# Contracting the last 64 channels over 128 rows in a split-precision MLP and DFT chain

## The chip, the cores and the metric

The kernel runs on one NeuronCore of a Trainium2 chip. The metric is the device time of one execution in microseconds. Engines are named as in the profile: PE is the matmul engine (PEld its weight loads), DVE, ACT and POOL are the vector, scalar and GpSimd engines, SP issues most of the DMAs.

## The reference

The program is a chain of three blocks over 2 batches, 768 tokens and 320 channels (8 heads of 40).

```
attention:  gated linear recurrence over 768 steps, 8 heads x 40   -> x [2, 768, 320]
block 1:    h = relu(x^T w_tok1) w_tok2 ;  u = x + h^T
            out1 = u + relu(u w_ch1) w_ch2          w_ch1 [320, 1536], w_ch2 [1536, 320]
block 2:    u = x + real(fft(fft(x, tokens), channels))
            un = layernorm(u) ;  out = u + relu(un w_ch1) w_ch2     w_ch1 [320, 1280]
```

Weights are handed over as float64 bits.

## The kernel before, in words

**Number format.** Every product that matters is done with each operand split in two: a high part rounded to 12 bits and a low part, the rest. A product is then three matmuls, high by high, high by low and low by high; low by low is left out. The weight words are decoded and split on the chip: `decode` (lines 73 to 87) is one ACT and three DVE instructions on a piece, `split` (94 to 99) adds one ACT copy that rounds to the high part and one POOL subtraction that gives the low part. The pool of decoded pieces has three buffers.

**The 320 channels as contraction rows.** 320 is 128 + 128 + 64. The activations of two token tiles (256 tokens) are transposed on PE and split by `transpose2` (409 to 425) into `uT`, five slots of 128 rows by 256 columns: slots 0 and 1 are the high parts of channels 0 to 255, slots 2 and 3 their low parts; slot 4 holds the high parts of channels 256 to 319 in rows 0 to 63 and their low parts in rows 64 to 127. The weight pieces of class `FF1` (110 to 136) have three row tiles; the third is rows 256 to 319 of the matrix twice, one copy above the other. So one matmul of 128 rows, high weights twice against slot 4, gives high by high and high weight by low activation together. The third term, low weight by high activation, needs 64 rows only. `split` forms the low part of that third row tile for rows 0 to 63 alone (`rows=64` from `FF1.conv`, line 126), and `mlp_hidden` (428 to 447) issues as the last of each group of eight matmuls one that contracts over 64 rows, `g(2, 1, ff, 64)` against `uT[0:64, 4, :]` (line 442).

**Loops.** Each of the two MLPs works on six sets of two token tiles, three per batch. A set is `mlp_hidden`, groups of eight matmuls of 256 columns, one group for each 128 hidden features (12 in block 1, 10 in block 2), two groups to a PSUM bank `phid`; `relu_split` (390) turns a bank into the high and low halves of `hid` with one ACT and one DVE instruction; then `mlp_out` (449) contracts `hid` with `w2` for each token tile, 36 or 30 matmuls of 320 columns into `pout`, all of 128 rows. In all there are 2 x 3 x 12 + 2 x 3 x 10 = 132 groups of eight. The DFT along the channels (`dft_stage`, 490 to 522) uses the same slots: for each of 3 tile pairs of each batch there are two groups of eight matmuls, the last of which contracts over 64 rows (line 515), 12 such groups. Its cosine and sine tables come as one constant, 128 rows high; slot 5 of it, the low parts of rows 256 to 319, fills rows 0 to 63 and is zero below (line 825).

**Order.** The generators `ch_stage`, `moe2_stage`, `dft_stage` and `attn_batch` yield estimated durations; `merge` emits a side stage under a main one (attention of batch 1 under the first MLP stage, the DFT of batch 0 under the second, that of batch 1 under the third), and a scheduler then orders each engine's instructions by its own simulated times. The order on each engine is fixed in the program: an engine waits at an instruction whose input is late, whatever stands behind it. PSUM pool `pmm` has four banks, shared by `phid`, `pout` and others. The weights of block 1 are decoded while its first set runs; those of block 2's first matrix (`v1`) under block 1's second stage, as their raw words land; those of its second matrix (`v2`) reuse the buffers of block 1's `w2` and can be loaded only as these come free.

Of the kernel before, what the change touches and what calls it, by code (L numbers as in the profile page):

```python
# [21 lines left out]
DM = H * D  # L22
# [16 lines left out]
def body(ctx, tc, io, out):  # L39
# [29 lines left out]
    def mm(o, l, r, a, z):  # L69
        nc.tensor.matmul(o, l, r, start=a, stop=z)  # L70

# [1 line left out]
    def decode(raw, n, dst=None):  # L73
        """float32 of the n float64 words in raw: the sign, the exponent less 896, 23 bits."""
        z = pz.tile([128, RAW], F32, tag="z", name="z")
        wi = raw.bitcast(I32).rearrange("p (n two) -> p n two", two=2)
        wf = raw.bitcast(F32).rearrange("p (n two) -> p n two", two=2)
        hw, lw = wi[:, :n, 1], wi[:, :n, 0]
        zi = z.bitcast(I32)[:, :n]
        nc.scalar.activation(z[:, :n], wf[:, :n, 1], AF.Copy, scale=2.0 ** -112)  # L80
        nc.vector.tensor_scalar(hw, hw, -2147483648, None, op0=ALU.bitwise_and)  # L81
        nc.vector.scalar_tensor_tensor(  # L82
            hw, zi, 3, hw, op0=ALU.logical_shift_left, op1=ALU.bitwise_or)
        o = zi if dst is None else dst.bitcast(I32)
        nc.vector.scalar_tensor_tensor(  # L85
            o, lw, 29, hw, op0=ALU.logical_shift_right, op1=ALU.bitwise_or)
        return z[:, :n]
# [3 lines left out]
        dma(raw, src)  # L91
        return raw

    def split(pool, tag, raw, n, rows=128):
        z = decode(raw, n)
        w = pool.tile([128, 2, n], F32R, tag=tag, bufs=1, name="w")
        nc.scalar.activation(w[:, 0, :], z, AF.Copy)  # L97
        nc.gpsimd.tensor_tensor(w[:rows, 1, :], z[:rows], f(w[:rows, 0, :]), op=ALU.subtract)  # L98
        return w

    def tok_load(i):
# [6 lines left out]
        decode(raw, RAW, tokw[:, i * RAW:(i + 1) * RAW])  # L108

    class FF1:  # L110
        """[DM, nf] in pieces: three row tiles (the third is rows 256.. twice) by RAW columns."""

        def __init__(self, pool, tag, src, nf):
            self.pool, self.tag, self.src = pool, tag, src
# [8 lines left out]

        def conv(self, i):
            k = self.keys[i]
            self.w[k] = split(self.pool, f"{self.tag}_{i}", self.raw.pop(k), self.n[k[0]],
                              64 if k[1] == 2 else 128)

        def ensure(self, ff):
            while len(self.w) < len(self.keys) and self.keys[len(self.w)][0] <= 128 * ff:  # L130
                self.conv(len(self.w))

        def get(self, kt, hl, ff, rows=128):
            o = 128 * ff
            s = o // RAW * RAW
            return self.w[s, kt][:rows, hl, o - s:o - s + 128]

    class FF2:
        """[nk * 128, DM] in pieces of 128 rows."""

        def __init__(self, pool, tag, src, nk):
            self.pool, self.tag, self.src, self.nk = pool, tag, src, nk
# [12 lines left out]
        def get(self, hl, k):  # L155
            return self.w[k][:, hl, :]

# [1 line left out]
    def gates(early, bcast, loadg):  # L159
        gt = ph.tile([128, 6144], F32R, tag="hid", name="gt")  # L160
        g = f(gt)
# [82 lines left out]

        return store

# [1 line left out]
    def attn_init(pa, pas):  # L248
        st = {}
        st["C"] = [pa.tile([128, 4, 2 * V41], F32, tag=f"C{i}", bufs=1, name=f"C{i}")  # L250
# [21 lines left out]
        st[b, c][2] = Dt  # L272

    def attn_chunk(pa, pas, st, b, c):
        """Yields in stages so that chunks can be pipelined."""
        kvo, kq, Dt, *pg = st[b, c]
        k3 = kvo[:, 0:DM].rearrange("p (h d) -> p h d", d=D)
        v3 = kvo[:, DM:DM + H * V41].rearrange("p (h d) -> p h d", d=V41)
# [126 lines left out]
            mm(p, tk2[:, m, 128 * t:128 * t + 128], hs[:, m, :], m == 0, m == 1)  # L405
        nc.vector.tensor_tensor(us[b][:, t, :], us[b][:, t, :], p, op=ALU.add)

# [1 line left out]
    def transpose2(ta, tb, pool=pu, tag="uT", bufs=2):  # L409
        uT = pool.tile([128, 5, 256], F32R, tag=tag, bufs=bufs, name="uT")  # L410
        pp, tg = late.get("pt", (pmm, "mm"))
# [12 lines left out]
            uT[64:128, 4, :], p2[0:64, 0:256], f(uT[0:64, 4, :]), op=ALU.subtract)  # L424
        return uT

# [1 line left out]
    def mlp_hidden(uT, wt, nff, w2=None):  # L428
        hid = ph.tile([128, 12, 2, 256], F32R, tag="hid", name="hid")
        for f2 in range(nff // 2):  # L430
            wt.ensure(2 * f2 + 4)
            if w2 is not None:
                w2.ensure(2 * (f2 - nff // 2 + 2))
            p = pmm.tile([128, 512], F32, tag="mm", name="phid").rearrange(
                "p (k n) -> p k n", k=2)
            for q in range(2):
                ff = 2 * f2 + q
                g = wt.get
                ops = [(g(0, 0, ff), uT[:, 0, :]), (g(1, 0, ff), uT[:, 1, :]),
                       (g(0, 1, ff), uT[:, 0, :]), (g(1, 1, ff), uT[:, 1, :]),  # L440
                       (g(0, 0, ff), uT[:, 2, :]), (g(1, 0, ff), uT[:, 3, :]),
                       (g(2, 0, ff), uT[:, 4, :]), (g(2, 1, ff, 64), uT[0:64, 4, :])]
                for i, (l, r) in enumerate(ops):
                    mm(p[:, q, :], l, r, i == 0, i == 7)
            relu_split(hid[:, 2 * f2:2 * f2 + 2, 0, :], hid[:, 2 * f2:2 * f2 + 2, 1, :], p)
            yield 1740
        return hid
# [38 lines left out]
            for i in range(2):  # L486
                yield from mlp_out(hid, W2, 12, us[b][:, ORDER[k][i], :], i)

# [1 line left out]
    def dft_stage(b, pf, pfs):  # L490
        cds, css, alt, odd = late["cds"], late["css"], late["alt"], late["odd"]
        n0 = NS + 2 * NJ
# [11 lines left out]
        for i in range(3):  # L504
            eT = eo(i)
            yield 700
            p = pfs.tile([128, 512], F32, tag="f", name="pf1")
            no = NS + NJ if i == 0 else NS
            for o, lsl, r0, n in ((0, 128, 0, no), (no, 0, NS, NJ)):
                ls = slice(lsl, lsl + 128)  # L510
                rs = slice(r0, r0 + n)
                ops = [(eT[:, 0, ls], cds[:, 0, rs]), (eT[:, 1, ls], cds[:, 1, rs]),
                       (eT[:, 2, ls], cds[:, 0, rs]), (eT[:, 3, ls], cds[:, 1, rs]),
                       (eT[:, 0, ls], cds[:, 2, rs]), (eT[:, 1, ls], cds[:, 3, rs]),
                       (eT[:, 4, ls], cds[:, 4, rs]), (eT[0:64, 4, ls], cds[0:64, 5, rs])]
                for q, (l, r) in enumerate(ops):
                    mm(p[:, o:o + n], l, r, q == 0, q == 7)
            nn = no + NJ
            nc.scalar.activation(AB[i][:, 0, 0:nn], p[:, 0:nn], AF.Copy)
            nc.vector.tensor_tensor(  # L520
                AB[i][:, 1, 0:nn], p[:, 0:nn], f(AB[i][:, 0, 0:nn]), op=ALU.subtract)
            yield 1800
# [15 lines left out]
        for k in range(3):  # L538
# [32 lines left out]
            nc.gpsimd.tensor_tensor(u[:, k, :], u[:, k, :], mx[:, 0:DM], op=ALU.add)  # L571
            nc.gpsimd.tensor_tensor(u[:, 3 + k, :], u[:, 3 + k, :], r2, op=ALU.add)
            yield 2100
        # layer norm statistics
        mv = pf.tile([128, 6, 2], F32, tag="mv", bufs=2, name="mv")
        for t in (0, 3, 1, 4, 2, 5):
            bs = pf.tile([128, 6], F32, tag="bs", bufs=2, name="bs")
# [45 lines left out]
            pass  # L623

    def merge(main, side, mt, sd, fns=()):
        """Emit main; spread side and the small jobs evenly beneath it."""
        tm_, ts_, nf = 0.0, 0.0, 0
        done = False
        for w in main:
            tm_ += w  # L630
            fr = tm_ / mt
            while not done and ts_ < fr * sd:
                try:
                    ts_ += next(side)
                except StopIteration:
                    done = True
            while nf < len(fns) and nf < fr * len(fns):
                fns[nf]()
                nf += 1
        if not done:  # L640
            drain(side)
        while nf < len(fns):
            fns[nf]()
            nf += 1
# [4 lines left out]
    pw = pmm.tile([128, 512], F32, tag="mm", name="pwarm")  # L649

    def warm(n):
        """Keeps the tensor engine's clock up where it would idle."""
        for _ in range(n):
            mm(pw[:, 0:256], wt[:, 0:128], wt, True, True)

    # ================= program =================
    warm(16)
    pa_cm = tc.tile_pool(name="pa", bufs=2)
    pa = pa_cm.__enter__()
# [143 lines left out]
def _constants():  # L803
    c = {}
    c["ident"] = np.eye(128, dtype=np.float32)
    sel = np.zeros((B, 4, 2, 2, B, 4), np.float32)
    for b in range(B):
        for r in range(4):
            for j in range(2):
                sel[b, r, j, j, b, r] = 1.0  # L810
    c["sel"] = sel.reshape(16, 16)
    d = np.arange(DM, dtype=np.float64)[:, None]
    cd = np.zeros((DM, NJ))
    sd = np.zeros((DM, NS))
    j = np.arange(NS + 1)
    cd[:, :NS + 1] = np.cos(2 * np.pi * ((d * j) % DM) / DM)
    j = np.arange(1, NS)
    sd[:, :NS - 1] = np.sin(2 * np.pi * ((d * j) % DM) / DM)
    hi, lo = _hl(np.concatenate([sd, cd], 1))
    n = NS + NJ  # L820
    cds = np.zeros((128, 6, n), np.float32)
    cds[:, 0], cds[:, 1] = hi[0:128], hi[128:256]
    cds[:, 2], cds[:, 3] = lo[0:128], lo[128:256]
    cds[0:64, 4], cds[64:128, 4] = hi[256:], hi[256:]
    cds[0:64, 5] = lo[256:]
    k = np.arange(384)
    a = 2 * np.pi * ((k[:, None] * k[None, :]) % S) / S
    cs, ss = np.cos(a), np.sin(a)
    cs[0, :] = (k % 2 == 0)
    ss[0, :] = 0.0  # L830
    css = np.zeros((128, 4, 3, 384), np.float32)
    for q, m in ((0, cs), (2, ss)):
        hi, lo = _hl(m)
        css[:, q] = hi.reshape(3, 128, 384).transpose(1, 0, 2)
        css[:, q + 1] = lo.reshape(3, 128, 384).transpose(1, 0, 2)
    alt = np.zeros((128, 256), np.float32)
    alt[:, 0] = 1.0 - 2.0 * (np.arange(128) % 2)
    alt[0, 128:] = np.arange(128) % 2
    c["dft"] = np.ascontiguousarray(
        np.concatenate([css.reshape(128, -1), alt, cds.reshape(128, -1)], 1))  # L840
    c["idx"] = np.ascontiguousarray((_slots()[384:] - 384).reshape(3, 128).T.astype(np.int32))
    return c
# [57 lines left out]
```

## Time and profile before

| what | us |
|---|---|
| median of 3 runs | 464.22 (463.49 to 472.81) |
| span of the profiled execution | 465.3 |
| PE busy in it | 453.8 |
| DVE busy in it | 248.1 |
| ACT busy in it | 158.1 |
| POOL busy in it | 112.0 |

The profile is one execution of the program with a record for each instruction. Of that execution the page gives the span, from the first to the last instruction, which is 1.1 us above the median time of the runs; sums are made against the span and then moved by that difference. A group of instructions stands on one line by code line, engine, operation, tiles and shape; the program's matmuls all go through one helper (line 70), so they are told apart by their tiles. Ends of matmuls are modelled, and a matmul's recorded duration overlaps its neighbour's, so how fast PE goes is read from the distance between starts. Some matmul records are missing.

### The profile page before, as it was taken

To read this page: it belongs to the slowest core of one execution; us is meant where nothing else is said; L and a number is where in the kernel's file an instruction comes from. 1 tells how busy PE (TensorE), PEld (TensorE's weight loads), DVE (VectorE), ACT (ScalarE), POOL (GpSimd) and SP (SyncE) were. 2 spreads that over 40 slices of the span, in tenths; PEclk is the share of its full clock that TensorE was granted. 3 is DMA by queue.
4 is the path that set the end of the run, shared out by engine and by line. 5 is a ranking of instruction groups with operands and counts; after the bars stand their busy time and mean duration, and the time that the engine had idled before them with its cause. 6 is when DMAs were issued, how large, how long until landed. Compare 5 with 4: busy or idle time off the path is not lost.

```text
span 465.3 us, 8110 instructions
## 1 busy us (share of the span) xinstructions
PE 453.8 (98%) x3254; PEld 391.8 (84%) x3254; DVE 248.1 (53%) x515; ACT 158.1 (34%) x382; POOL 112.0 (24%) x131
## 2 busy tenths in 40 slices
PE   9899998999999999999999999979999999999996
PEld 7789876888889889778988998968989989797986
DVE  8656779899844232165892425288534235312221
ACT  2766635596454020033462212145122021202020
POOL 5574347486511002001240210022201110000000
PEclk9965599999999999999999999989999999999999
DMA  7558659933320001059100000340000000000000
GB/s 217 188 186 278 226 186 356 334 140 117 117 89 1 14 16 43 15 189 394 57 3 0 2 1 0 96 187 1 14 15 1 30 1 28 1 28 1 30 1 28
DMA packets 15669, 42.27 MB, mean 91 GB/s; under 512 B 2080, under 2 KB 4992, under 8 KB 15504
## 3 DMA queue, kind: packets, MB, share of 16 engines
q1 hardware_dynamic: 15200, 37.30, 23.6%
q0 software_dynamic: 432, 4.46, 2.4%
q8 instruction: 25, 0.41, 0.4%
q14 instruction: 12, 0.10, 0.1%
HBM read 38.76 MB, written 3.00 MB: 90 GB/s over the span
## 4 chain that ended last, share of the span: by engine, by line
PE 91%; DMA 4%; DVE 3%; issue 1%; ACT 1%; SPq 0%; DVEq 0%; ACTq 0%
PE phid L70 38%; PE pout L70 25%; PE pf L70 6%; PE ps L70 5%; PE py L350 4%; PE py L327 3%; PE pt L70 2%; PE ptr L416 2%; PE h L70 2%; DMA kq<-in_kqT_dram 1%; DMA tkr<-in_tok_dram 1%; DMA raw<-in_v_dram 1%; PE kv L70 1%; PE pwarm L70 1%; PE ptr L419 1%
## 5 line engine op out<-in xcount | busy, mean ns | idle before, releaser
L70 PE MATMUL phid<-uT,w 128*128 128x256 f32 (+1 forms) x1056 | 182.8, 308 | 3.6 <-ACT uT L420 3.6
L70 PEld LDWEIGHTS phid<-uT,w 128*128 128x128 f32 (+1 forms) x1056 | 145.0, 190 | 36.2 <-ACT uT L420 4.3
L70 PE MATMUL pout<-w,hid 128*128 128x320 f32 x792 | 126.2, 313 | 0.0
L70 PEld LDWEIGHTS pout<-w,hid 128*128 128x128 f32 x792 | 116.5, 188 | 2.7
L392 DVE SCALAR_TENSOR_TENSOR hid<-phid,hid 128x512 fp32r<-128x512 f32 x66 | 45.5, 690 | 77.3 <-ACT hid L391 77.1
L391 ACT ACTIVATE hid<-phid 128x512 fp32r<-128x512 f32 x66 | 39.4, 598 | 133.3 <-PE phid L70 131.2
L98 POOL TENSOR_TENSOR w<-z,w 128x320 fp32r<-128x320 f32 (+4 forms) x46 | 46.3, 1016 | 89.3 <-ACT w L97 89.2
L459 DVE TENSOR_TENSOR us<-us,pout 128x320 f32<-128x320 f32 x24 | 11.6, 486 | 51.6 <-PE pout L70 51.5
L97 ACT ACTIVATE w<-z 128x320 fp32r<-128x320 f32 (+2 forms) x46 | 22.0, 481 | 22.8 <-DVE z L85 22.8
L85 DVE SCALAR_TENSOR_TENSOR z<-raw 128x320 int32<-128x320 int32 (+2 forms) x46 | 29.4, 640 | 0.7
L70 PE MATMUL ps<-kq 40*128 40x128 f32 x192 | 29.5, 340 | 0.0
L80 ACT ACTIVATE z<-raw 128x320 f32<-128x320 f32 (+2 forms) x46 | 22.9, 505 | 17.8 <-DMA raw<-in_v_dram 11.9
L82 DVE SCALAR_TENSOR_TENSOR raw<-z,raw 128x320 int32<-128x320 int32 (+2 forms) x46 | 28.3, 623 | 0.4
L70 PEld LDWEIGHTS ps<-kq 40*128 40x128 f32 x192 | 24.5, 232 | 2.8 <-issue 2.1
L302 ACT ACTIVATE Dt<-Dt,tm 128x128 f32<-128x128 f32 x80 | 25.1, 393 | 0.1
L81 DVE TENSOR_SCALAR raw<-raw 128x320 int32<-128x320 int32 (+2 forms) x46 | 21.6, 473 | 6.6 <-ACT z L80 6.5
L571 POOL TENSOR_TENSOR us<-us,mx 128x320 f32<-128x320 f32 x6 | 5.5, 921 | 73.4 <-DVE mx L559 73.4
L303 POOL TENSOR_SCALAR_AFFINE_SELECT Dt<-Dt 128x512 f32<-128x512 f32 x24 | 17.9, 752 | 11.3 <-ACT Dt L302 11.2
L319 DVE TENSOR_TENSOR Dt<-Dt,ps 128x512 f32<-128x512 f32 x24 | 16.1, 679 | 7.6 <-PE ps L70 5.6
L70 PE MATMUL pwarm<-wt 128*128 128x256 bf16 x116 | 18.5, 320 | 1.1 <-DVE wt L647 1.1
L350 PEld LDWEIGHTS py<-kvo,Dt 128*64 128x64 f32 x384 | 16.2, 166 | 3.4 <-issue 2.0
L420 ACT ACTIVATE uT<-ptr 128x512 fp32r<-128x512 f32 x18 | 10.7, 594 | 24.6 <-PE ptr L416 23.5
(120 smaller groups left out, 433.3 us busy)
## 6 DMA issues: line engine op xcount, KB each, us to landing
kvo<-in_kvo_dram SPq DMA_DIRECT2D x12, 484.0 KB
Dt<-Gd SPq DMA_DIRECT2D x10, 512.0 KB
raw<-in_w_dram SPq DMA_DIRECT2D x12, 384.0 KB
kq<-in_kqT_dram SPq DMA_DIRECT2D x24, 160.0 KB
raw<-in_w_dram SPq DMA_DIRECT2D x12, 320.0 KB
raw<-in_v_dram SPq DMA_DIRECT2D x9, 384.0 KB
dc<-in_dft_dram POOLq DMA_DIRECT2D x1, 3398.0 KB, 12.9
raw<-in_v_dram SPq DMA_DIRECT2D x10, 320.0 KB
```

The source lines that it names most:

```text
L70: nc.tensor.matmul(o, l, r, start=a, stop=z)
L80: nc.scalar.activation(z[:, :n], wf[:, :n, 1], AF.Copy, scale=2.0 ** -112)
L81: nc.vector.tensor_scalar(hw, hw, -2147483648, None, op0=ALU.bitwise_and)
L82: nc.vector.scalar_tensor_tensor(hw, zi, 3, hw, op0=ALU.logical_shift_left, op1=ALU.bitwise_or)
L85: nc.vector.scalar_tensor_tensor(o, lw, 29, hw, op0=ALU.logical_shift_right, op1=ALU.bitwise_or)
L97: nc.scalar.activation(w[:, 0, :], z, AF.Copy)
L98: nc.gpsimd.tensor_tensor(w[:rows, 1, :], z[:rows], f(w[:rows, 0, :]), op=ALU.subtract)
L302: nc.scalar.activation(Dt[:, h, :], G4[j][:, r, :], AF.Exp, bias=nu[:, h:h + 1])
L303: nc.gpsimd.affine_select(D4[:, j], D4[:, j], pattern=[[0, 4], [1, L]], compare_op=ALU.is_ge, fill=0.0, base=0, channel_multiplier=-1)
L350: nc.tensor.matmul(py[64 * q:64 * q + 64, h, :], Dt[:, h, 64 * q:64 * q + 64], v3[:, h, :], start=c == 0 and h == 0, stop=True, skip_group ...
L391: nc.scalar.activation(hi, ps, AF.Relu)
L392: nc.vector.scalar_tensor_tensor(lo, ps, 0.0, f(hi), op0=ALU.max, op1=ALU.subtract)
```

## The change

The third row tile's low part is formed for all 128 rows, so that both copies of the low weights are there, and the last matmul of each group of eight contracts over 128 rows: low weights twice against slot 4. That adds low weight by low activation for the last 64 channels. The DFT does the same; its constant gets the low table in rows 64 to 127 too. Comments and docstrings go as well; these are left out below.

```diff
-    def split(pool, tag, raw, n, rows=128):
+    def split(pool, tag, raw, n):
         z = decode(raw, n)
         w = pool.tile([128, 2, n], F32R, tag=tag, bufs=1, name="w")
         nc.scalar.activation(w[:, 0, :], z, AF.Copy)
-        nc.gpsimd.tensor_tensor(w[:rows, 1, :], z[:rows], f(w[:rows, 0, :]), op=ALU.subtract)
+        nc.gpsimd.tensor_tensor(w[:, 1, :], z, f(w[:, 0, :]), op=ALU.subtract)
...
-            self.w[k] = split(self.pool, f"{self.tag}_{i}", self.raw.pop(k), self.n[k[0]],
-                              64 if k[1] == 2 else 128)
+            self.w[k] = split(self.pool, f"{self.tag}_{i}", self.raw.pop(k), self.n[k[0]])
...
-        def get(self, kt, hl, ff, rows=128):
+        def get(self, kt, hl, ff):
             o = 128 * ff
             s = o // RAW * RAW
-            return self.w[s, kt][:rows, hl, o - s:o - s + 128]
+            return self.w[s, kt][:, hl, o - s:o - s + 128]
...
-                       (g(2, 0, ff), uT[:, 4, :]), (g(2, 1, ff, 64), uT[0:64, 4, :])]
+                       (g(2, 0, ff), uT[:, 4, :]), (g(2, 1, ff), uT[:, 4, :])]
...
-                       (eT[:, 4, ls], cds[:, 4, rs]), (eT[0:64, 4, ls], cds[0:64, 5, rs])]
+                       (eT[:, 4, ls], cds[:, 4, rs]), (eT[:, 4, ls], cds[:, 5, rs])]
...
-    cds[0:64, 5] = lo[256:]
+    cds[0:64, 5], cds[64:128, 5] = lo[256:], lo[256:]
```

## Rows read from the trace of the kernel before

**Rows 1.** Page: busy time by engine; granted PE clock in 40 slices, in tenths.
```profile
PE 453.8 (98%) x3254; PEld 391.8 (84%) x3254; DVE 248.1 (53%) x515; ACT 158.1 (34%) x382; POOL 112.0 (24%) x131
...
PEclk9965599999999999999999999989999999999999
```

**Rows 2.** Page: the chain of work that ended last, share of the span by engine.
```profile
PE 91%; DMA 4%; DVE 3%; issue 1%; ACT 1%; SPq 0%; DVEq 0%; ACTq 0%
```

**Rows 3.** Groups of PE by shape: line, operation, tiles, shapes, count | busy us, mean ns.
```profile
L70 PE MATMUL phid<-uT,w 128*128 128x256 f32 x924 | 149.2, 298 | 3.6 <-ACT uT L420 3.6
...
L70 PE MATMUL phid<-uT,w 64*128 64x256 f32 x132 | 49.9, 379 | 0.0
...
L70 PE MATMUL pf<-dc,uT 64*128 64x162 f32 x6 | 2.0, 338 | 0.0
```

**Rows 4.** Timeline of PE around one group's end: start us, us, what, how many.
```profile
440.10 0.28 PE L70 MATMUL phid<-uT,w 128*128 128x256 f32 x1
...
440.30 0.70 PE L70 MATMUL phid<-uT,w 64*128 64x256 f32 x2
...
440.62 0.51 PE L70 MATMUL phid<-uT,w 128*128 128x256 f32 x2
...
440.84 0.53 PE L70 MATMUL phid<-uT,w 128*128 128x256 f32 x3
```

**Rows 5.** Timeline of PE: one whole set of ten groups and what follows.
```profile
416.64 13.29 PE L70 MATMUL phid<-uT,w 128*128 128x256 f32 x80
429.86 0.66 PE L416 MATMUL ptr<-ident,un 128*128 128x128 f32 x4
```

**Rows 6.** Timeline of PE: a run in which all matmuls have 128 rows.
```profile
393.81 3.10 PE L70 MATMUL phid<-uT,w 128*128 128x256 f32 x24 [0.58 <-ACT uT L420]
396.75 0.60 PE L416 MATMUL ptr<-ident,un 128*128 128x128 f32 x4
```

**Rows 7.** Timeline of PE: DFT along channels (first pair), along tokens (second pair).
```profile
233.66 2.25 PE L70 MATMUL pf<-dc,uT 128*128 128x160 f32 x14
235.84 0.41 PE L70 MATMUL pout<-w,hid 128*128 128x320 f32 x1
...
251.57 2.72 PE L70 MATMUL pf<-AB,dc 128*128 128x162 f32 x20
254.12 0.32 PE L70 MATMUL phid<-uT,w 128*128 128x256 f32 x1
```

**Rows 8.** Groups of POOL by shape, the subtraction that gives the low weights.
```profile
L98 POOL TENSOR_TENSOR w<-z,w 128x384 fp32r<-128x384 f32 x14 | 15.7, 1130 | 20.4 <-ACT w L97 20.4
...
L98 POOL TENSOR_TENSOR w<-z,w 64x384 fp32r<-64x384 f32 x7 | 8.1, 1164 | 19.4 <-ACT w L97 19.4
```

**Rows 9.** Stretches: busy us of PE, PEld, DVE, ACT, POOL; PEclk, DMA share, GB/s.
```profile
76.20:123.00 46.80, 46.80 (x376) 38.84 (x374) 44.58 (x78) 32.53 (x84) 30.59 (x33) 1.00 0.61 211
221.50:245.00 23.50, 23.50 (x158) 21.31 (x157) 20.60 (x43) 12.20 (x29) 8.91 (x10) 1.00 0.06 21
304.70:329.00 24.30, 23.36 (x141) 20.48 (x142) 22.34 (x44) 12.72 (x30) 8.18 (x9) 0.93 0.14 55
```

**Rows 10.** Matmuls on `phid` in 76.2:129, 202.7:245 and 304.7:329, with their forms.
```profile
L70 PE MATMUL phid<-uT,w x129: 274/282/522, 76.2 to 128.8; 128*128 128x256 f32 x113, 64*128 64x256 f32 x16
...
L70 PE MATMUL phid<-uT,w x139: 277/282/522, 202.7 to 244.5; 128*128 128x256 f32 x122, 64*128 64x256 f32 x17
...
L70 PE MATMUL phid<-uT,w x80: 274/284/457, 305.6 to 323.9; 128*128 128x256 f32 x70, 64*128 64x256 f32 x10
```

**Rows 11.** Timeline of ACT at 220; in brackets idle before and what ended it.
```profile
220.26 0.60 ACT L391 ACTIVATE hid<-phid 128x512 fp32r<-128x512 f32 x1 [2.68 <-PE phid L70]
220.75 1.42 ACT L80 ACTIVATE z<-raw 128x384 f32<-128x384 f32 x3
```

**Rows 12.** Waits of 304.7:329 (us, times, longest); the chain after that wait.
```profile
PE phid L70 <- ACT uT L420: 3.0, 1, 3.0
...
305.64 3.66 PE phid L70 x16
```

## Prediction

> **What bounds the kernel now.** I read the page first: PE is busy for 453.8 of 465.3 us, DVE for 248.1, and the PE clock is granted in full in nearly every slice [rows 1]. A busy PE need not be a fast one, so the chain of waits comes next: 91% of the chain that ended last is PE's own work [rows 2]. The time is therefore the sum of the distances between the starts of PE's instructions, and the question is what those distances are. The groups by shape show that the 132 matmuls with 64 rows are not cheaper than their 924 neighbours with 128 rows and the same 256 columns: their mean is 379 ns against 298 [rows 3]. These durations are modelled, so I went to the timeline of single instructions. A 128-row matmul starts at 440.10, the 64-row one at 440.30, the next 128-row one at 440.62 and the one after that at 440.84, after which three share 0.53 us [rows 4]. Steps of 0.20, 0.32 and 0.22 us stand around every 64-row matmul. What a step is without one is seen in a run where the scheduler put 24 matmuls of 128 rows together: from 393.81 to the next instruction at 396.75 [rows 6], 2.94 us. That run has one slow step of the 0.22 kind, after its wait; without the 0.10 it has too much, a step is 2.84 / 24 = 0.118 us.
>
> The same rows speak on the cause. The first slow step, 0.20 us, lies inside a group, between its seventh and eighth matmul; no new PSUM region begins there, only the row count changes. The run of 24, the first six matmuls of each of four groups, crosses three group starts without the excess. So I put the excess down to the row count, not to the group's end.
>
> **The change part by part, with costs.**
>
> *The eighth matmul of each MLP group gets 128 rows.* A set of ten groups takes 429.86 - 416.64 = 13.22 us, 1.322 a group [rows 5]. Eight steps of 0.118 are 0.944. The difference is 0.378 us; 132 groups [rows 3] give **49.9 us**. All of it lies on PE, which sets the end wherever nothing else is late. In a few places the matmul behind a group belongs to attention and has few rows too, and some of the change of shape would stay; I don't price that apart.
>
> *The eighth matmul of each DFT group.* Two groups take 235.84 - 233.66 = 2.18 us for 16 matmuls [rows 7]. The nearest run without the 64-row ones is the DFT along tokens, 20 matmuls in 254.12 - 251.57 = 2.55 us, 0.128 a step [rows 7]; it holds two matmuls of a single row, so this is an upper bound for a clean step, and 16 x 0.128 = 2.04 leaves 0.07 us a group. The upper bound of the saving is the MLP's 0.378. I take 0.17, nearer the lower end because the row is the DFT's own and its steps fall to about 0.115 once a quarter of a microsecond for the single-row pair is taken out: 12 x 0.17 = **2.0 us**, with ends of 0.8 and 4.5.
>
> *The subtraction on POOL covers 128 rows instead of 64.* Seven instructions of 64 rows have a mean of 1164 ns, fourteen of 128 rows 1130 [rows 8]: nothing. POOL waits for ACT before them, and that idle time covers them.
>
> *The constant* has the same size; zeros become numbers. No DMA changes. *No wait is added:* the seventh matmul of a group already reads all 128 rows of slot 4, so the eighth finds them there, and its low weights come from one instruction as before.
>
> So PE's own sum is 51.9 us. **What is late next** decides how much of it arrives. PE then meets instructions whose inputs come from DVE, and in three stretches DVE has little air [rows 9]:
>
> *76.2 to 123, decoding block 1's weights:* DVE is busy for 44.58 of 46.80 us. 16 groups end in and just behind it [rows 10], worth 6.0. DVE's order is fixed and its work unchanged, so it can end earlier by no more than its idle 2.2. I keep 2.0 and lose **4.0**.
>
> *304.7 to 329, decoding v2:* DVE is busy for 22.34 of 24.30. Ten groups and two DFT groups are worth 4.1; I keep the idle 2.0 and lose **2.1**. The 3.0 us wait just before, for ACT's copy of `uT` [rows 12], has none of the changed matmuls on its way and stays; likewise the 16 steps of 3.66 / 16 = 0.23 us behind it, in a stretch with a mean granted clock of 0.93.
>
> *221.5 to 245, decoding v1:* DVE is busy for 20.60 of 23.50. Up to there 17 groups and four DFT groups are worth 7.1. Here the decoding itself starts earlier, because its first ACT instruction at 220.75 stands behind a relu at 220.26 that waited 2.68 us for PE [rows 11]. Earlier start and 2.9 of air cover nearly all; I lose **1.0**.
>
> Everywhere else DVE, ACT and POOL have room: in a PE-only set a bank's relu costs 0.60 on ACT [rows 11], and two groups will still take 1.9 us.
>
> Sum: 51.9 - 4.0 - 2.1 - 1.0 = 44.8 us. Against the profiled span that is 465.3 - 44.8 = 420.5; the median of the runs lies 1.1 below the span, so **419.4 us**.
>
> **Rivals.**
>
> *All of it arrives.* The three stretches lose nothing, because the waits of DVE there were for PE after all: 464.2 - 51.9 = 412, and 410 with the DFT at its upper end. The almost full DVE speaks against it. Chance 0.13.
>
> *DVE takes back all that lies in its three stretches.* 6.0 + 4.1 + 7.1 = 17.2 lost; 51.9 - 17.2 = 34.7, which gives 429.5. For it: fixed orders, three decode buffers, four PSUM banks. Against it: the later start of the v1 decoding is PE's doing. Chance 0.20.
>
> *The row count costs nothing, and nothing changes.* The slow steps would belong to the group's rhythm and stay: 464. Against it is the slow step inside the group and the clean run of 24 [rows 4, 6]. Chance 0.03. The Trainium skill's page "TensorE: Matmul & The Clock Gate", in "Why this matters for your kernels", says that a single matmul of 32 rows takes the same time as one of 128, by which swapping one for the other would give this 464; the trace disagrees as far as neighbours go, with steps of 0.20 and 0.32 us against 0.118. Its page "TensorEngine Tiling (Array Packing)", "Key Properties", says that a change of tiling mode drains the engine, which is the side that the steps of rows 4 take.
>
> *Slower: PE's new waits bring its clock down.* Its place is the decoding from 76 to 129, where PE would now stop several times for DVE. After the one long wait of the trace, the steps went from 0.118 to 0.23 us for 16 matmuls [rows 6, 12], 1.8 us. To eat 44.8 us and 2% of 464 more, 9.3, such steps would have to number 54.1 / 0.11 = 490, that is more than 30 such waits, or a clock that does not come back over six sets. The trace shows one long wait, and the clock back within 4 us. It would then be 474 or more. Chance 0.02.
>
> **How the numbers follow.** The forecast has 0.62. The range goes from 411, nearly all of the sum, to 431, past the case where DVE takes its three stretches back; it leaves out no change, slower, and the ends of the others. A measurement of this kernel tells about 2% from no change, so faster has the forecast and the first two rivals, 0.95; same 0.03; slower 0.02.
>
> **What would show it.** Right: no 64-row forms are left; a set of 80 matmuls of `phid` takes 9.4 to 9.8 us instead of 13.2, and this holds in each of the last three sets; `pout` keeps its step. Between 76 and 129 PE shows idle time released by ACT or DVE, and the stretch shrinks by 2, not by 6; between 305 and 329 likewise. Wrong: a group of eight that still holds a step of 0.2 or 0.3; idle PE in the final sets; another order of PE's instructions, which could move any of the three stretches by some microseconds either way.

## The result, and the profile after

The changed kernel takes 418.13 us (median of 5, 416.06 to 429.8) against 464.22 before (463.34 to 472.81): a ratio of 0.896 with a 95% interval of 0.889 to 0.903, 46.1 us by the medians. 419.4 was predicted, with a range of 411 to 431. Here and below a median is over all runs of a kernel and a ratio over the fast ones alone, so the two can differ a little.

The profile taken with the result is of an execution of 429.8 us, 11.7 above the median, and what it lost is told below; so the rows of after are from a second profile of the same kernel (`e1_again`), of 417.6 us. First its page: busy time by engine, the granted PE clock in 40 slices, the chain that ended last.

```profile
PE 405.5 (97%) x3254; PEld 377.6 (90%) x3254; DVE 246.4 (59%) x515; ACT 157.6 (38%) x382; POOL 111.0 (27%) x131
...
PEclk9975559998999999999999999998999999999999
...
PE 84%; DMA 10%; DVE 2%; issue 1%; SPq 1%; ACT 1%; ACTq 0%
```

PE still makes the chain, but less of it than the 91% before [rows 2]: DMA has grown. The groups by shape, then on the timeline the same kind of whole set as in [rows 5], and the same DFT run as in [rows 7]:

```profile
L70 PE MATMUL phid<-uT,w 128*128 128x256 f32 x1056 | 137.7, 286 | 3.4 <-ACT uT L419 3.3
```

```profile
395.53 9.63 PE L70 MATMUL phid<-uT,w 128*128 128x256 f32 x80
404.99 0.46 PE L70 MATMUL pout<-w,hid 128*128 128x320 f32 x2
...
220.88 1.77 PE L70 MATMUL pf<-dc,uT 128*128 128x160 f32 x14
222.49 0.34 PE L70 MATMUL pout<-w,hid 128*128 128x320 f32 x1
```

There is one form left, and 80 matmuls go from start to next start in 9.46 us instead of 13.22: 0.376 us less for each group. The DFT's run goes from 2.18 to 1.61. On POOL the subtraction for the third row tile has merged into the others, at 1155 ns against 1130 and 1164 [rows 8]:

```profile
L98 POOL TENSOR_TENSOR w<-z,w 128x384 fp32r<-128x384 f32 x21 | 23.9, 1155 | 34.1 <-ACT w L97 34.1
```

The time by stage, cut at the starts of matmuls that both traces have. "By steps" is 0.376 for each MLP group and 0.33 for each DFT group (`e3_dft_only` below).

| from, to | groups | before | after | shorter | by steps |
|---|---|---|---|---|---|
| start, first `phid` | 0 | 76.2 | 76.4 | -0.2 | 0 |
| to the last `pout` of the first set | 16 | 51.2 | 49.8 | 1.4 | 6.0 |
| to the first `h` of batch 1 | 20 | 61.5 | 55.1 | 6.4 | 7.5 |
| to the first `pf` | 12 | 35.6 | 31.2 | 4.5 | 4.5 |
| to block 2's first transpose | 24 + 6 DFT | 77.3 | 66.3 | 11.0 | 11.0 |
| to its first one of batch 1 | 30 + 6 DFT | 90.6 | 77.5 | 13.1 | 13.3 |
| to the end | 30 | 72.9 | 61.4 | 11.5 | 11.3 |
| sum | 132 + 12 | 465.3 | 417.6 | 47.7 | 53.6 |

From the first `h` of batch 1 on everything arrives. What was lost, 5.7 us, was lost in block 1's first stage, the second and third row of the table.

### The profile page after: what moved, and what is told of

Read it like the earlier page. It is cut to its first block, busy times and chain, and to the rows that moved or that the text cites. A ratio compares the mean times of both kernels' runs of the same rounds, so it can differ in the third digit from the quotient of the medians.

```text
span 428.1 us, 8110 instructions
## 1 busy us (share of the span) xinstructions
PE 409.3 (96%) x3254; PEld 380.7 (89%) x3254; DVE 247.1 (58%) x515; ACT 157.2 (37%) x382; POOL 112.7 (26%) x131
## 4 chain that ended last, share of the span: by engine, by line
PE 81%; DMA 8%; DVE 3%; issue 2%; POOL 1%; ACT 1%; SPq 1%; DVEq 0%; POOLq 0%; ACTq 0%
PE pout L70 27%; PE phid L70 25%; PE ps L70 6%; PE pf L70 6%; DMA raw<-in_v_dram 4%; PE py L349 4%; PE py L326 3%; PE h L70 2%; PE ptr L415 2%; DMA tkr<-in_tok_dram 2%; PE pt L70 2%; DMA kq<-in_kqT_dram 1%; PE pwarm L70 1%; PE kv L70 1%; POOL w L98 1%
## 5 line engine op out<-in xcount | busy, mean ns | idle before, releaser
L70 PE MATMUL phid<-uT,w 128*128 128x256 f32 x1056 | 137.9, 286 | 2.3 <-ACT uT L419 2.3
L70 PEld LDWEIGHTS phid<-uT,w 128*128 128x128 f32 x1056 | 130.8, 192 | 4.5 <-ACT uT L419 2.8
L70 PEld LDWEIGHTS pout<-w,hid 128*128 128x128 f32 x792 | 118.1, 190 | 2.3 <-DVE uT L420 0.8
L98 POOL TENSOR_TENSOR w<-z,w 128x320 fp32r<-128x320 f32 (+2 forms) x46 | 47.0, 1032 | 82.7 <-ACT w L97 81.1
L70 PE MATMUL ps<-kq 40*128 40x128 f32 x192 | 31.3, 355 | 0.0
L70 PEld LDWEIGHTS ps<-kq 40*128 40x128 f32 x192 | 25.7, 243 | 3.4 <-issue 2.1
L85 DVE SCALAR_TENSOR_TENSOR z<-raw 128x320 int32<-128x320 int32 (+2 forms) x46 | 28.3, 617 | 0.7
L349 PE MATMUL py<-kvo,Dt 128*64 128x41 f32 x384 | 19.3, 264 | 0.0
```

What stands on the lines that cost most here:

```text
L85: nc.vector.scalar_tensor_tensor(o, lw, 29, hw, op0=ALU.logical_shift_right, op1=ALU.bitwise_or)
L98: nc.gpsimd.tensor_tensor(w[:, 1, :], z, f(w[:, 0, :]), op=ALU.subtract)
L349: nc.tensor.matmul(py[64 * q:64 * q + 64, h, :], Dt[:, h, 64 * q:64 * q + 64], v3[:, h, :], start=c == 0 and h == 0, stop=True, skip_group ...
```

## The experiments

**`e1_again`: the changed kernel, a second profile.**

> The changed kernel again, unaltered, for a second profile. Theory (the steps around each 64-row matmul are gone, and part of the gain is lost where PE now meets late DVE work): 414 to 420 us; a set of 80 matmuls of phid in about 9.5 us; idle PE in the three decoding stretches. If the 5.6 us stop of PE near 215 us in the first profile (behind the decoding of v1, whose words landed after the DFT constant) belongs to the kernel, it stands here too; if it was chance of that execution, it is under 1 us.

422.8 us as the median of 4 (418.4 to 431.3), on a chip on which the kernel before took 477.2. The stop near 215 us belongs to some executions. In the first profile ACT (first two rows) waits 9.23 us for a piece of v1, and PE (last two) stops for 5.37:

```profile
203.77 0.56 ACT L80 ACTIVATE z<-raw 128x384 f32<-128x384 f32 x1 [1.11 <-DMA raw<-in_v_dram]
213.56 0.54 ACT L80 ACTIVATE z<-raw 128x384 f32<-128x384 f32 x1 [9.23 <-DMA raw<-in_v_dram]
...
204.00 6.35 PE L70 MATMUL phid<-uT,w 128*128 128x256 f32 x51
215.71 1.09 PE L415 MATMUL ptr<-ident,eo 128*128 128x128 f32 x4 [5.37 <-DVE uT L420]
```

In the second profile the first two pieces come together, and PE doesn't stop:

```profile
199.24 1.24 ACT L80 ACTIVATE z<-raw 128x384 f32<-128x384 f32 x2 [1.15 <-DMA raw<-in_v_dram]
...
199.42 6.35 PE L70 MATMUL phid<-uT,w 128*128 128x256 f32 x51
205.61 0.60 PE L415 MATMUL ptr<-ident,eo 128*128 128x128 f32 x4
```

The stage from `h` to `pf` takes 38.5 us in the one and 31.2 in the other. In the first profile the DFT constant's packets began at 202.5, before v1's first piece was in at 203.4, and the second piece was in only at 213.5, when the constant's last packet had ended (212.9); from 204 to 211 the DMA engines moved 99 packets of the constant, of 27,184 bytes each, and 100 of v1, of 3,072 each. In the second profile both pieces were in by 199.9, and the constant, begun at 199.0, delayed only those behind them. (The first profile lost another 4.6 us ahead of the first `phid`, where nothing was changed.)

**`e2_mlp_only` and `e3_dft_only`: either half of the change.**

```diff
# e2: after, with
+ (eT[:, 4, ls], cds[:, 4, rs]), (eT[0:64, 4, ls], cds[0:64, 5, rs])]
# e3: before, with
+ (eT[:, 4, ls], cds[:, 4, rs]), (eT[:, 4, ls], cds[:, 5, rs])]
+ cds[0:64, 5], cds[64:128, 5] = lo[256:], lo[256:]
```

> The change in the MLPs alone; the eighth matmul of the 12 DFT groups keeps its 64 rows. Theory of the sum: slower than the changed kernel by the DFT's term, 2.0 us (ends 0.8 and 4.5), so about 419 to 420. Rival: the DFT groups run in the shadow of other waits and the difference is 0.

> The change in the DFT along the channels alone: 12 groups. Theory of the sum: 2.0 us less than before (ends 0.8 and 4.5), each pf run of 16 matmuls 0.3 to 0.6 us shorter. Rival (the saved steps turn into waits): no change in the time, the runs of pf shorter all the same.

The DFT alone: 464.13 us against 467.24, ratio 0.990 (0.983 to 0.997), a difference too small for the time alone to tell. The run of [rows 7] is as short as in the changed kernel:

```profile
234.32 1.77 PE L70 MATMUL pf<-dc,uT 128*128 128x160 f32 x14
235.93 0.34 PE L70 MATMUL pout<-w,hid 128*128 128x320 f32 x1
```

The stage from the first `pf` to block 2's first transpose takes 75.3 us instead of 77.3: 2.0 for six groups, 0.33 each, 4.0 for the twelve. So the saved steps did not turn into waits, which was the rival. `e2_mlp_only` says the same from the other side: 68.3 us there against 66.3. Its median, 427.7, is no measure of the DFT: its profile has the stop at v1 (37.7 us from `h` to `pf`).

**`e4_pairs`: all 64-row matmuls kept, set side by side in pairs.**

```diff
+                if q == 1:
+                    ops = ops[7:] + ops[:7]
```

> The kernel before, with all its 64-row matmuls kept, but in each second group of a bank the 64-row matmul comes first, so that two of them stand side by side: 66 changes of row count and back instead of 132. Theory (each change of row count and back costs 0.378 us): 66 x 0.378 = 25 us less than before, 439, or 442 where the decoding takes some back. Rival (the cost belongs to each 64-row matmul itself, or to the end of a group): 464, no change.

446.2 us against 477.2, ratio 0.943 (0.932 to 0.954): 31 us less by the medians, 27 by the ratio, with all 132 matmuls of 64 rows still there. First the group of the 64-row matmuls; then, on the timeline, a whole set, which takes 11.56 us, in the middle between the 13.29 of [rows 5] and the 9.63 above, and one pair:

```profile
L70 PE MATMUL phid<-uT,w 64*128 64x256 f32 x132 | 33.5, 332 | 0.0
```

```profile
419.11 11.56 PE L70 MATMUL phid<-uT,w 128*128 128x256 f32 x80
...
420.03 0.39 PE L70 MATMUL phid<-uT,w 64*128 64x256 f32 x1
...
420.46 0.39 PE L70 MATMUL phid<-uT,w 128*128 128x256 f32 x1
```

From 420.03 to 420.46 there are two 64-row matmuls, 0.43 us, which is what one takes with the slow step behind it [rows 4] and a clean one of 0.12. So the cost goes with the change of row count and back, not with the matmul, nor with the end of a group, of which there are as many as before. The rival is refuted.

**`e5_rows96`: the eighth matmul over 96 rows.**

```diff
+                              96 if k[1] == 2 else 128)
+                       (g(2, 0, ff), uT[:, 4, :]), (g(2, 1, ff, 96), uT[0:96, 4, :])]
```

> The kernel before, but the eighth matmul of each MLP group contracts over 96 rows (the low weights formed for 96 rows, the low activations of 32 channels come in as well); the DFT as before. If any row count other than 128 brings the slow steps: 464. If it is 64 rows in particular, half the array: as the changed kernel without the DFT's part, 418 to 421.

428.2 us as the median of 4 (422.4 to 433.4), beside 422.8 for the changed kernel on the same chip; its DFT still has the 64-row matmuls, worth 4.0 us. The whole set is as fast as with 128 rows:

```profile
401.39 9.68 PE L70 MATMUL phid<-uT,w 128*128 128x256 f32 x80
410.91 0.89 PE L70 MATMUL pout<-w,hid 128*128 128x320 f32 x5
```

9.52 us from start to next start. A row count other than 128 is not enough to bring the slow steps: 96 rows run with 128, and 64 do not.

The weight loads (PEld) show what goes with the slow steps. Between matmuls of one row count a weight load starts 0.116 us (the median) ahead of its own matmul, while the one before still runs. In the kernel before, at each of 237 changes between 128 and 64 rows in `phid` it starts together with its own matmul; here are the loads of the two matmuls at 440.30 and 440.62 of [rows 4]:

```profile
440.30 0.18 PEld L70 LDWEIGHTS phid<-uT,w 64*128 64x128 f32 x1
...
440.61 0.19 PEld L70 LDWEIGHTS phid<-uT,w 128*128 128x128 f32 x1
```

With 96 rows the loads start 0.117 us ahead, as between full ones. The Trainium skill's page "TensorEngine Tiling (Array Packing)", "Key Properties", names a drain at a change of tiling mode, and its section "Available Configurations" has modes of 64 and 32 rows but none of 96; these sets agree with it. The page gives no price; here it is 0.376 us.

**`e10_odd128`: the single-row matmuls of the DFT along the tokens over 128 rows.**

```diff
-                mm(pP, odd[0:1, :], AB[0][0:1, hl, NS:NS + NJ], False, hl == 1)
+                mm(pP, odd, AB[0][:, hl, NS:NS + NJ], False, hl == 1)
```

> The changed kernel, and the last pair of matmuls of another kind with few rows made full: in the DFT along the tokens two matmuls in each of six groups contract over a single row; here they contract over 128 rows, of which the table's other 127 are zero, so that the result is the same. If the cost lies in the change of row count, whatever the number: each group of 20 matmuls loses the steps of about 0.20, 0.18 and 0.20 us for three of 0.11, so 2.3 us instead of 2.55, and 1.5 us less in all. If it belongs to 64 rows alone: 2.55 us and no change.

The run of [rows 7], second pair:

```profile
243.19 2.39 PE L70 MATMUL pf<-AB,dc 128*128 128x162 f32 x20
245.42 0.44 PE L70 MATMUL phid<-uT,w 128*128 128x256 f32 x2
```

2.23 us instead of 2.55, and 0.32 less in each of the six such runs: 1.9 us less on PE. The cost isn't that of 64 rows alone. The median, 419.9 us, can't tell 1.9 us.

**`e7_after_nosign` and `e8_before_nosign`: a lighter decoding, which leaves out the weights' sign, in the changed kernel and in the one before.**

```diff
-        nc.vector.tensor_scalar(hw, hw, -2147483648, None, op0=ALU.bitwise_and)
-        nc.vector.scalar_tensor_tensor(
-            hw, zi, 3, hw, op0=ALU.logical_shift_left, op1=ALU.bitwise_or)
+        nc.vector.tensor_scalar(hw, zi, 3, None, op0=ALU.logical_shift_left)
```

> The changed kernel with a lighter decoding: the weights' sign is left out, so that two DVE instructions on a piece are left of three. To be read against the kernel before with the same lighter decoding. Theory (in the stretch from the first phid matmul to the end of the first set's pout DVE's decoding holds back PE, which is why only 1.4 of 6.0 us arrived there): with the lighter decoding that stretch is 4 to 6 us shorter here than in the kernel before with it. Rival (something else holds PE there, POOL's subtraction, the DMA of the words or PSUM): the difference of the two stays near 1.4 us.

> The kernel before with the same lighter decoding (the weights' sign left out). Theory: PE sets its time already, so it gains less from the lighter DVE than the changed kernel does, 0 to 3 us of 464 in the stages after the first phid matmul. Rival: both gain alike.

424.4 us (411.2 to 428.0) and 465.9 (456.8 to 471.7), beside 469.0 for the kernel before. What counts here is the stretch from the first `phid` to the first set's last `pout`, as in [rows 9]: before, the changed kernel, the changed kernel with the lighter decoding, and before with it.

```profile
76.21:127.36 51.15, 51.15 (x411) 42.51 (x410) 47.70 (x83) 33.23 (x85) 31.76 (x34) 1.00 0.58 202
```

```profile
76.42:126.19 49.77, 48.62 (x411) 42.74 (x410) 47.74 (x83) 33.20 (x85) 31.40 (x34) 0.97 0.59 198
```

```profile
81.87:121.42 39.55, 37.18 (x334) 33.65 (x334) 34.43 (x60) 30.89 (x81) 25.00 (x30) 1.00 0.64 219
```

```profile
81.59:124.55 42.96, 41.37 (x333) 34.94 (x334) 33.73 (x60) 30.59 (x81) 24.61 (x30) 1.00 0.62 206
```

DVE is busy for 93 and 96% of the first two. With the lighter decoding the change is worth 42.96 - 39.55 = 3.4 us there instead of 1.4: under the 4 to 6 that the theory wanted, above the rival's 1.4. The scheduler also put fewer matmuls into the stretch (333 instead of 411), so the fairer figure goes on to the first `h` of batch 1: 113.1 us in the kernel before and 102.8 in the changed one, 10.3 shorter, where it was 112.7 to 104.9, 7.8 shorter. DVE's decoding thus holds some 2.5 of the 5.7 us lost, by one profile of each (2.2, if the 104.6 of `e2_mlp_only` is taken, in which the clock stayed up as in these two); it does not hold all of it. The kernel before gains nothing there from the lighter DVE (113.1 against 112.7), as the theory had it.

**`e9_again` and `e6_v1_later`: the stop at v1.** The second pins the decoding to a later place; the load stays.

```diff
+        ld = nc.scalar.activation(z[:, :n], wf[:, :n, 1], AF.Copy, scale=2.0 ** -112)
+        if late.get("pin"):
+            tc.keep_in_program_order(ld)
...
+    merge(ct, dft0(), 69000, 20000, [lambda: None] * 3 + [lambda i=i: conv_v1(i) for i in range(len(V1.keys))])
```

> The changed kernel unaltered, beside the one with v1 decoded later. Theory: its executions fall into two kinds about 7 us apart, by whether the second v1 piece lands before the DFT constant or behind it; in the profile the first DFT matmul comes 31 us behind the end of attention's last stage in the one kind and 37 to 38 in the other. Rival (a general slowing of this chip): one broad spread without such a gap.

> The changed kernel with the decoding of v1 pinned to a later place in the program, behind the first DFT tiles; nothing is left out. Theory (the stop of PE near 210 us is ACT waiting, in its fixed order, for a v1 piece that the DFT constant's DMA has overtaken; the relus stand behind it and PE runs out of PSUM banks after four of them): that stop is gone in every execution, from the end of batch 1's token mixing to the first DFT matmul it takes some 26 to 31 us, never 37; the times lie closer together and at or below the lower ones of the changed kernel, 412 to 418. Rival (the stop is DVE's load of decoding, whenever it comes): the same microseconds are lost later in that stage, and the time is that of the changed kernel.

419.8 us (415.1 to 423.7) and 418.4 (417.3 to 423.7): no difference. The changed kernel's times do not fall into two clean kinds; as times, the rival's broad spread is what came. Both profiles took 31.2 us from `h` to `pf`, and both then 66.3 to block 2's first transpose, so the later decoding costs nothing, and the rival (the same load lost later) is refuted. With it ACT's first v1 instruction comes at 226.56, after the first DFT tiles, and waits for nothing:

```profile
212.34 0.60 ACT L392 ACTIVATE hid<-phid 128x512 fp32r<-128x512 f32 x1 [1.96 <-PE phid L70]
218.65 0.57 ACT L520 ACTIVATE AB<-pf 128x484 fp32r<-128x484 f32 x1 [5.71 <-PE pf L70]
...
226.56 0.55 ACT L80 ACTIVATE z<-raw 128x384 f32<-128x384 f32 x1
```

The other profiles show which executions stop. In the first one, `e2`, `e7` and `e10` the second piece of v1 is in 12 to 13 us after its load was issued, behind most of the constant, and from `h` to `pf` it takes 37.3 to 38.5 us; in `e1`, `e5` and `e9` it is in after less than 4 us, and it takes 31.2. In the two profiles with the later decoding, this one and `e11_both`, the piece is late as well, in after 10.5 and 11.0 us, and from `h` to `pf` it takes 31.2 all the same. So the DMA still comes late in this version, and PE no longer stops for it.

**`e11_both`: v1 decoded later and the single-row matmuls full.**

> The same, with v1 decoded later. Theory: as the version with v1 decoded later less 1.5 us; from the end of attention's last stage to the first DFT matmul 31 us. Rival: no better than the changed kernel.

415.7 us (410.8 to 422.5), ratio 0.883 (0.876 to 0.891) to the kernel before, where `e10_odd128` beside it had 0.895 (0.890 to 0.900). Its profile has 31.2 us from `h` to `pf` and runs of 2.19 us. It is the fastest version measured; from the changed kernel (0.896, 0.889 to 0.903, on another chip) it is not clearly apart.

## Why the prediction was right

**The step of 0.378 us for each MLP group: right.** 0.376 measured, in every undisturbed set, and `e4_pairs` and `e5_rows96` show the cause that rows 4 and 6 had suggested.

**The DFT's term: mis-sized, by a misread row.** 2.0 us were taken, between ends of 0.8 and 4.5; it is 4.0. The working counts 16 matmuls in the 2.18 us of [rows 7]; the row has 14. No record is missing, `pf` has 96 of them for 6 x 16; the other two of this pair stand earlier:

```profile
231.40 0.35 PE L70 MATMUL pf<-dc,uT 128*128 128x160 f32 x2
```

With 14 the same rows give (2.18 - 14 x 0.128) / 2 = 0.19 us a group as the lower end, above the 0.17 that was taken. `e10_odd128` then takes the single-row pair apart: without it the run's step is 2.23 / 20 = 0.112, which gives 0.31 a group, 3.7 us for the twelve.

**The decoding at 76 to 123: right in size, in part by other causes.** 4.0 us were to be lost to DVE; 4.6 were. PE's instructions stand in the same order in both traces, so the steps can be set side by side. 1.2 us of the 4.6 are two waits of PE, one for DVE and one for POOL:

```profile
PE pout L70 <- DVE uT L420: 0.7, 1, 0.7
PE kv L70 <- POOL kw L287: 0.4, 1, 0.4
```

1.5 us are a lowered clock, as in the rival that was called slower: behind the first of these waits 13 of 18 matmuls of `pout` ran at half the clock. Before, and in the second profile with the stretch around:

```profile
96.69 2.90 PE L70 MATMUL pout<-w,hid 128*128 128x320 f32 x18
```

```profile
95.12 4.44 PE L70 MATMUL pout<-w,hid 128*128 128x320 f32 x18 [0.68 <-DVE uT L420]
```

```profile
94.90:105.00 10.10, 9.88 (x93) 9.07 (x93) 9.99 (x18) 9.64 (x30) 8.97 (x11) 0.83 0.24 88
```

Most of the rest are slow steps that stayed, which is told under "not priced". DVE stands close behind PE all the same: in `e2_mlp_only`, with the same order and the clock at 1.00 throughout, PE instead waits for DVE once more, and the stretch takes 49.5 us, hardly less than 49.8:

```profile
PE ps L70 <- DVE Dt L318: 0.9, 1, 0.9
```

In `e9_again` the clock fell a little later and for longer, and the stretch took 54.0 us instead of 49.8 (in `e10_odd128` 53.9):

```profile
105.00:116.00 11.00, 10.20 (x39) 8.29 (x40) 10.19 (x22) 5.38 (x15) 5.45 (x6) 0.59 0.21 76
```

So the clock does fall in this stretch in some executions. That PE's new waits bring it down is not shown: in `e3_dft_only`, which has the kernel before's code here, it fell to half at 105.6 without a wait of PE (52.6 us, granted clock 0.97), and in `e2_mlp_only` it stayed up behind both of the waits above and the third. (The working's 1.8 us for one fall divides a duration, 3.66; from start to next start, 305.64 to 309.10, the 16 steps took 3.46, which makes it 1.6.) The rival was rightly held far below what would turn the sign.

**The decoding of v2 at 305 to 329: wrong.** 2.1 us were to be lost and 0.2 were, in a stage that holds more besides. I equated what DVE can gain with what PE can. DVE's last decoding did come only 1.8 us earlier, counted from block 2's first transpose (328.12 - 301.83 against 303.22 - 278.76), so the bound held for DVE. But the last run of `pout` stood 3.7 us behind it before (331.82) and stands 0.7 behind it now (303.92): PE ate 3.0 us of slack that the busy share doesn't show.

**The decoding of v1: wrong in kind.** 1.0 us was to be lost; it is 0 or about 7, by whether a DMA lands first. That race was in no term, because the kernel before hid it: with 2 x 1.322 us a bank, four PSUM banks covered 10.6 us, more than the 9.2 of that wait, and with 2 x 0.946 they cover 7.6 (argued from the traces; the kernel before was not caught in such an execution).

**Not priced:** where a group stands next to attention the change of mode stays. The prediction named this and put no number on it. The stage from 128 us on lost 1.1 of 7.5 us. Set side by side, 17 of its 20 groups, with a 128-row matmul behind them, save 0.38 us each; the two with a `ps` of 40 rows behind them save nothing, and the one with a `py` of 64 weight columns 0.19. That is nearly all of the 1.1. In the stage before, two groups of 16 have a `ps` behind them and save nothing either.

**The sum.** Between the two profiles 47.7 us were saved, against 44.8 in the working. Three terms made the saving too small, by 4.9 (2.0 in the DFT, 1.9 at v2, 1.0 at v1), and two too large, by 1.7 (0.6 at 76 to 123, 1.1 not priced). So part of the closeness is errors that cancel; the bulk of it is the MLP's term, which was right with its cause.

## What to carry to other kernels

In this kernel a matmul over 64 rows or over one was not cheaper than a full one, and between full ones it brought three slow steps: 0.38 us for 64 rows, three times the 0.12 of a full matmul. Look for such ones and fill them with duplicates or zeros, or at least put the short ones side by side. Count the matmuls in the row that you divide by. Read the cost from the distances between starts, in the nearest run that lacks the odd instruction. What a faster bound engine gives back is read from the slack between a result and its first use, not from the busy share of the engine that makes it, and from transfers that the slower kernel covered.

## What the runs showed of the hardware

96 rows go with 128 without a slow step (9.52 us a set against 9.46), 64 rows and one row do not. At a change between 128 and 64 rows the weight load starts with its own matmul instead of 0.116 us ahead of it, at all 237 such changes of `phid` in the kernel before. Two 64-row matmuls in a row show no extra cost for the second beyond a step of 0.12 us in their sum. While the constant's transfer and v1's ran together, the DMA engines moved as many packets of the one (99 of 27,184 bytes) as of the other (100 of 3,072), so v1 got a tenth of the bytes. In one execution 13 matmuls of `pout` ran at half the clock behind a wait of PE of 0.68 us (18 took 4.3 us instead of 2.7 to the next start); the same wait in `e2_mlp_only` was followed by none at a lowered clock.
